# A planned attention and two-layer kernel: longer assumed delays for its loads, and the x2 stores of layer 1 begun by GpSimd

## The chip, the cores and the metric

The kernel runs on one core of a Trainium2 chip. The metric is the device time of one execution in microseconds. Engines are called as the profile calls them: PE is TensorE (matrix products), DVE is VectorE, ACT is ScalarE, POOL is GpSimd, SP is SyncE, which only begins transfers (DMAs).

## The reference

Causal attention in blocks of 64 rows over 4 batches, 8 heads, 576 positions and a head size of 64 gives 2304 tokens of 512 numbers. Two layers follow, each a product with a 512 x 2048 matrix, a function of each element, and a product with a 2048 x 512 matrix. All is in float32.

```python
scores = scale * np.matmul(q, k.transpose(0, 1, 3, 2))
mask = block_i >= block_j            # blocks of 64 positions
scores = np.where(mask, scores, -1000000000.0)
attn = np.exp(scores - np.max(scores, axis=-1, keepdims=True))
attn = attn / (np.sum(attn, axis=-1, keepdims=True) + 1e-09)
x = np.matmul(attn, v)               # then heads side by side: [2304, 512]
# layer 1
h = x @ moe_w_in
g = np.where(h >= 1, h, np.where(h <= -1, 0.0, (h + 1) ** 2 / 4))
x = g @ moe_w_out
# layer 2
h = x @ moe2_w_in
out = (h * np.cos(h)) @ moe2_w_out
```

## The kernel before

The work has three stages on PE: attention (to about 160 us), layer 1 (to 557 us), layer 2. Each float32 product of a layer is made of three products in a shorter form: an operand is split into a high and a low part (a copy that rounds, then a subtraction, the helpers cp and diff, lines 189 to 191 and 185).

Attention goes through 16 pairs of heads, in periods of two pairs. Q, K and V are loaded by SP, scores are computed in units (S3, S2, S0 and "tl" for the last 64 rows of two pairs), DVE takes the maximum (line 598) and prepares the divisor (lines 621 and 625), ACT the exponential, and POOL divides (line 635); PE turns the result (line 692) and multiplies it with V (line 727, then the halves, 738). Beside it the weights of layer 1 are brought in: a raw load of 512 KB, then two steps "top" and "low" (ACT, the second also on POOL, line 290), a joining step on DVE (line 300), and the split into the two parts in tile m or n. Ten of these conversions lie in attention, at pairs 6 to 15.

Layer 1 runs over five blocks of tokens (four of 512, and the third of 256), each in 16 steps over the hidden dimension. A step has a first product (mm1, line 868, into h), four operations on ACT and DVE that make g (881, 882, 883 and its split), and a second product (mm2, line 909) into four accumulators called parts 0 to 3. The first product is issued two steps ahead of the second. At a block's last step each part is copied to the tile o, which has two buffers taken in turn (part % 2), and stored to x2d in memory by two DMAs of 128 KB (for the block of 256: one of 256 KB, line 925). So part 2 can be copied only when both stores of part 0 have landed, part 3 only after those of part 1, and the next block's second product needs the part's accumulator empty. In the same stage the weights of layer 2 are converted (w_combine: raw loads, top, low, join, sums of pieces on line 340, and stores of tiles o and f to w2i and w2o), and x_load fetches the next block's x (line 839).

What decides the order of all this: PE's order is written out by hand (OPENING, PERIOD, CLOSING, and the loop over steps). All else is put into a Plan. An operation has a cost per engine on which it may run, what it reads and writes, and a latency until its result counts as there. The plan simulates the engines and gives each operation to the engine and place where it could begin first; the instructions are then issued in exactly that order, and each engine works through its own in order. So a number in the plan sets no wait of its own; it changes the order, and with costs for several engines ("AV", "AG") who does the work. Latencies of transfers were 2.0 us everywhere:

```python
    def dma(kb, reads, writes, fn):
        do("S", 0.1 + kb / 230.0, reads, writes, lambda e: fn(), latency=2.0)
```

Of the kernel before, what the change touches and what calls it, by code (L numbers as in the profile page):

```python
# [102 lines left out]
def attn_moe_moe_kernel(ctx: ExitStack, tc: tile.TileContext, q, k, v, w_in1, w_out1, w_in2, w_out2, out):  # L103
    nc = tc.nc
    B, H, S, D = q.shape
# [4 lines left out]
    NB = 256  # L110
# [8 lines left out]
    KB = 1024  # L119
    pin = tc.keep_in_program_order  # L120
# [47 lines left out]
    x2d = [dram.tile([DM, NB], F32, name=f"x2d{j}") for j in range(NBLK)]  # L168
# [33 lines left out]
    def do(eng, cost, reads, writes, fn, lock="G", latency=0.0):  # L202
        plan.add(eng, cost, reads, writes, fn, lock, latency)
# [9 lines left out]
    def dma(kb, reads, writes, fn):  # L213
        do("S", 0.1 + kb / 230.0, reads, writes, lambda e: fn(), latency=2.0)

    def issue(count, kb, reads, writes, fn, rate=270.0):
        do("S", max(0.45 * count, kb / rate), reads, writes, lambda e: fn(), latency=2.0)

    def span(name, off, size):
        return [(name, b) for b in range(off // 512, (off + size + 511) // 512)]  # L220
# [40 lines left out]
    def raw_load(layer, f, which, slot, after=()):  # L261

        def emit():
            a = M.F1.view((8 + 4 * slot) * KB, [2 * DM], I32)
            w = srcs[layer][which].bitcast(I32)
            start = load_in_order if after else nc.sync.dma_start
            if which == 0:
                start(
                    out=a.rearrange("p (k f) -> p k f", k=NK),
                    in_=w[:, f * 256:(f + 1) * 256].rearrange("(k p) f -> p k f", p=128),  # L270
                )
            else:
                start(out=a, in_=w[f * 128:(f + 1) * 128, :])

        (issue if after else lambda _, *args: dma(*args))(1, 512, list(after), [("top", slot), ("low", slot)] + span("f", (8 + 4 * slot) * KB, 4 * KB), emit)

    def joined(slot, v, vk):

# [122 lines left out]
    for n in range(NK, N):  # L401
        b, h, _ = pairs[n]
# [79 lines left out]
    def raw_keys(n, which, parts=range(2)):  # L482
        return [("raw", which, raw_home(n, which), a) for a in (parts if n < PE_PAIRS[which] else [n % 2])]

    def load_v(n):
        src, t, hs = v[pairs[n][0]], M.V[n % 2], heads(n)

        def emit():
            for h in range(2):
                load_in_order(  # L490
                    out=t[:, 0:LAST, h, :], in_=src[pairs[n][1 + h], 0:128 * LAST, :].rearrange("(t p) d -> p t d", p=128)
                )
            o = slice(64 * (n % 2), 64 * (n % 2) + 64)
            load_in_order(out=t[o, LAST], in_=src[hs, 128 * LAST:S, :].rearrange("h p d -> p h d"))
            for x in range(2):
                at_ = 256 * x + 128
                load_in_order(
                    out=t[64:128, LAST + 1 + x], in_=src[hs, at_:at_ + 64, :].rearrange("h p d -> p h d")
                )

        issue(5, 358, [], [("V", n % 2)], emit, 205.0)

    def load(n, which, part=None):
        if n >= N:
            return
        if which == 2:
            return load_v(n)
        b, h0, h1 = pairs[n]
        src = (k, q)[which][b]
        t = M.R[which][raw_home(n, which)]  # L510
        if n < PE_PAIRS[which]:
            parts = range(2) if part is None else [part]
            c = slice(NTK * parts[0], NTK * parts[-1] + NTK)

            def emit():
                for h in range(2):
                    load_in_order(
                        out=raw_view(n, which)[:, c, h, :], in_=src[pairs[n][1 + h]].rearrange("(t p) d -> p t d", p=TK)[:, c],
                    )

            issue(2, 147 * len(parts), [], raw_keys(n, which, parts), emit, 205.0)
            return

        def emit():
            for x in range(4):
                g = src[h0 + 2 * (x // 2):h0 + 2 * (x // 2) + 2].rearrange("h t d -> (h t) d")
                load_in_order(
                    out=t[32 * x:32 * x + 32].rearrange("p (a d) -> p a d", d=32),
                    in_=g[:, 32 * (x % 2):32 * (x % 2) + 32].rearrange("(a r) d -> r a d", r=32),
                )  # L530

        issue(4, 590, [], raw_keys(n, which) + raw_keys(n + 1, which), emit, 140.0)

    def load_next(n, which):
        p = PE_PAIRS[which]
# [353 lines left out]
    def mm2(s, part):  # L889
# [29 lines left out]
        cp("AV", 512, y, a_of, [A], Y)  # L919
        if two:  # L920
            for c, j in enumerate(js):
                dma(128, Y, [("x2d", j, part)], lambda c=c, j=j: nc.sync.dma_start(
                    out=x2d[j][128 * part:128 * (part + 1)], in_=y()[:, NB * c:NB * (c + 1)]))
        else:
            dma(256, Y, [("x2d", js[0], part)], lambda: nc.sync.dma_start(
                out=x2d[js[0]][256 * part:256 * (part + 1)].rearrange("(k p) n -> p k n", p=128),
                in_=y().rearrange("p (k n) -> p k n", k=2),
            ))

    HT = 384  # L930
    AT = ({1: 0, 2: 1, 4: 2, 6: 3, 3: 4, 7: 5, 5: 6}, {1: 0, 2: 1, 3: 2, 5: 3, 7: 4, 4: 5, 6: 6})
# [567 lines left out]
```

## Time and profile before

| | |
|---|---|
| time, median of 3 runs | 919.14 us (916.41 to 920.05) |
| profiled execution | 918.29 us, its span 916.5 us |
| PE busy | 905.4 us, 99% |
| DVE, ACT, POOL busy | 71%, 62%, 17% |
| DMA issues of the x2 stores | 34, all by SP |
| raw weight loads of 512 KB, issue to landing (median) | 4.4 and 4.7 us |
| loads of V of 128 KB; of K and of Q of 144 KB (median) | 2.7; 4.3 and 3.1 us |
| x2 stores of 128 KB (median) | 1.8 us |

The span runs from the first to the last instruction; the profiled execution's time is 1.8 us longer. Times in the rows are counted from the start of the span.

### The profile page before, as it was taken

How to read it: one execution, taken by the hardware profiler on the slowest of the kernel's cores; microseconds unless marked ns; L12 is line 12 of the kernel's file. 1: busy time of each engine (PE TensorE's matmuls, PEld its weight loads, DVE VectorE, ACT ScalarE, POOL GpSimd, SP SyncE). 2: the span in 40 equal slices, each digit the busy share in tenths (PEclk: the TensorE clock that was granted, in tenths of full speed). 3: DMA queues.
4: the chain of work that ended last, by engine and by line, in shares of the span. 5: the costliest groups of instructions: out<-in, count | busy, mean ns of one | idle time of the engine just before them, and what ended most of it. 6: DMA issues, size and time to landing. Idle time of an engine off the chain costs nothing.

```text
span 916.5 us, 17951 instructions
## 1 busy us (share of the span) xinstructions
PE 905.4 (99%) x6834; PEld 811.5 (89%) x6834; DVE 655.3 (71%) x1041; ACT 564.3 (62%) x1060; POOL 159.2 (17%) x279
## 2 busy tenths in 40 slices
PE   8999999999999999999999999999999999999998
PEld 6778778888878889988888889999999999999998
DVE  6799997777856666666336224999959899388883
ACT  6978887897757656566445334776417674166641
POOL 3567775332101101202000000000000000000000
PEclk9999999999999999999999999999999999999999
DMA  7769865875766575575230506777897777877771
GB/s 154 147 131 210 184 177 166 256 241 175 255 235 218 198 240 206 182 257 207 81 114 24 207 30 225 253 250 250 275 348 254 254 249 257 292 259 253 247 263 61
DMA packets 159957, 189.92 MB, mean 207 GB/s; under 512 B 84608, under 2 KB 117888, under 8 KB 159872
## 3 DMA queue, kind: packets, MB, share of 16 engines
q1 hardware_dynamic: 159872, 188.78, 64.4%
q8 instruction: 54, 0.88, 0.4%
q14 instruction: 31, 0.25, 0.1%
HBM read 145.23 MB, written 43.52 MB: 206 GB/s over the span
## 4 chain that ended last, share of the span: by engine, by line
PE 88%; DVE 4%; SPq 2%; DMA 2%; ACT 2%; issue 1%; POOL 1%; ACTq 0%; POOLq 0%; DVEq 0%
PE a L909 19%; PE h L868 19%; PE q L1052 19%; PE q L1153 18%; PE t L692 3%; PE t L589 3%; PE t L727 3%; PE end L1153 2%; SPq L839 1%; SPq L123 1%; PE t L784 1%; DVE sm L598 1%; PE t L738 1%; DVE n L194 1%; PE t L655 1%
## 5 line engine op out<-in xcount | busy, mean ns | idle before, releaser
L1052 PE MATMUL q<-m 128*128 128x384 f32 x1008 | 175.2, 334 | 0.0
L1052 PEld LDWEIGHTS q<-m 128*128 128x128 f32 x1008 | 174.7, 188 | 0.1
L1153 PE MATMUL q<-m,n 128*128 128x256 f32 x1116 | 136.5, 283 | 0.0
L1153 PEld LDWEIGHTS q<-m,n 128*128 128x128 f32 x1116 | 135.2, 192 | 0.0
L909 PE MATMUL a<-g,m 128*128 128x512 f32 (+1 forms) x540 | 120.8, 372 | 3.6 <-ACT o L189 2.3
L883 DVE SCALAR_TENSOR_TENSOR f<-f,h 128x512 f32<-128x512 f32 (+1 forms) x80 | 50.5, 631 | 91.8 <-ACT f L882 91.5
L909 PEld LDWEIGHTS a<-g,m 128*128 128x128 f32 x540 | 95.2, 190 | 22.0 <-ACT o L189 3.0
L881 ACT ACTIVATE f<-h,half 128x512 f32<-128x512 f32 (+1 forms) x80 | 51.3, 641 | 83.9 <-PE h L868 83.6
L185 DVE TENSOR_TENSOR g<-f,g 128x512 fp32r<-128x512 f32 (+1 forms) x80 | 54.2, 678 | 30.1 <-ACT g L189 25.3
L868 PE MATMUL h<-m 128*128 128x512 f32 (+1 forms) x324 | 66.8, 355 | 0.0
L189 ACT ACTIVATE g<-f 128x512 fp32r<-128x512 f32 (+1 forms) x71 | 42.6, 600 | 33.8 <-DVE f L883 33.8
L868 PEld LDWEIGHTS h<-m 128*128 128x128 f32 x324 | 54.1, 189 | 8.6
L598 DVE TENSOR_REDUCE sm<-t 128x1 f32<-128x384 f32 (+7 forms) x128 | 50.4, 447 | 13.4 <-PE t L589 12.8
L300 DVE SCALAR_TENSOR_TENSOR f<-f 128x512 uint32<-128x512 uint32 x64 | 45.3, 712 | 17.0 <-ACT f L285 15.0
L635 POOL TENSOR_SCALAR n<-n,sm 128x64 f32<-128x64 f32 (+6 forms) x104 | 49.3, 497 | 32.4 <-ACT n L668 14.0
L1021 ACT ACTIVATE f<-f,hpi 128x768 f32<-128x768 f32 x48 | 44.6, 929 | 16.3 <-DVE f L1017 16.3
L868 PE MATMUL h<-x,m 128*128 128x512 f32 x216 | 52.6, 391 | 0.0
L909 PE MATMUL a<-g,n 128*128 128x512 f32 (+1 forms) x240 | 52.5, 368 | 0.0
L909 PEld LDWEIGHTS a<-g,n 128*128 128x128 f32 x240 | 42.1, 189 | 7.5
L868 PEld LDWEIGHTS h<-x,m 128*128 128x128 f32 x216 | 40.7, 190 | 8.4
L882 ACT ACTIVATE f<-f 128x512 f32<-128x512 f32 (+1 forms) x80 | 46.9, 586 | 1.7
L285 ACT ACTIVATE f<-f 128x512 f32<-128x512 f32 x64 | 42.8, 675 | 0.5 <-DMA f<-in_moe_w_in_dram 0.4
(143 smaller groups left out, 1642.4 us busy)
## 6 DMA issues: line engine op xcount, KB each, us to landing
m<-w2i SPq DMA_DIRECT2D x84, 512.0 KB, 4.2
m<-w2o SPq DMA_DIRECT2D x84, 512.0 KB, 3.7
f<-in_moe_w_out_dram SPq DMA_DIRECT2D x32, 512.0 KB, 4.4
f<-in_moe_w_in_dram SPq DMA_DIRECT2D x32, 512.0 KB, 4.7
w2i<-f SPq DMA_DIRECT2D x8, 1024.0 KB, 4.3
w2o<-f SPq DMA_DIRECT2D x8, 1024.0 KB, 4.2
w2i<-o SPq DMA_DIRECT2D x8, 768.0 KB, 3.4
w2o<-o SPq DMA_DIRECT2D x8, 768.0 KB, 4.4
```

Of the source, the lines that this page charges most:

```text
L185: return (eng or nc.vector).tensor_tensor(out=lo, in0=raw, in1=hi.bitcast(F32), op=ALU.subtract)
L300: pin(nc.vector.scalar_tensor_tensor(out=v().bitcast(U32), in0=t.bitcast(U32), scalar=3, in1=w.bitcast(U32), op0=ALU.logical_shift_left, o ...
L598: nc.vector.tensor_reduce(out=stat(0, n, i, i + 1), in_=pb(at_, a)[:, off:off + nk], axis=AX.X, op=ALU.max, negate=True,)))
L635: do("G", 0.25 + 0.00082 * w, sk(2, n, e0, e0 + 1) + [P_(i, n)], [writes], lambda e: pin(nc.gpsimd.tensor_scalar(out=out(), in0=probs(i, m ...
L868: pin(nc.tensor.matmul(out=h_of(), lhsT=wt[:, a, kk * 128:(kk + 1) * 128], rhs=x[:, b, 0:w], start=(kk == 0 and i == 0), stop=(kk == NK - ...
L881: nc.scalar.activation(out=g(), in_=h_of(), func=ACTF.Relu, bias=half, scale=0.5)))
L882: do("A", 0.05 + 0.00084 * w, E, E, lambda e: pin(nc.scalar.activation(out=g(), in_=g(), func=ACTF.Square)))
L883: do("V", 0.07 + w / 960.0, [H] + E, E, lambda e: pin(nc.vector.scalar_tensor_tensor(out=g(), in0=g(), scalar=1.0, in1=h_of(), op0=ALU.min ...
L909: pin(nc.tensor.matmul(out=o, lhsT=wt[:, a, dm:dm + 128], rhs=b, start=(f == 0 and i == 0 and c == 0), stop=(f == NF - 1 and i == 2), skip ...
L1021: nc.scalar.activation(out=o, in_=a, func=func, **kw)
L1052: pin(nc.tensor.matmul(out=ps[:, e, 0:HT], lhsT=w[:, e, a, 128 * kk:128 * (kk + 1)], rhs=L2.xq[i][:, kk, c], start=(not src and kk == 0 an ...
L1153: pin(nc.tensor.matmul(out=part(m), lhsT=t[:, e, a, 128 * m:128 * (m + 1)], rhs=w[:, e, o], start=(i not in (2, 3) and q == 0 and e == 0 a ...
```

## The change

Four numbers of the plan change: the latency that it counts for attention's loads of V goes from 2.0 to 2.5, that for the later loads of K and Q (four DMAs for two pairs) from 2.0 to 3.0, and that for raw weight loads of layer 1 that wait for a mark in attention from 2.0 to 5.0. The stores of x2 are begun by POOL in place of SP; the plan counts 0.9 us of POOL for each and a latency of 2.0, and they are fixed in the plan's order, which the stores on SP were not. As after.py has four lines more, its line numbers are 4 higher from line 276 on.

```diff
--- before.py
+++ after.py
@@ -213,8 +213,8 @@
     def dma(kb, reads, writes, fn):
         do("S", 0.1 + kb / 230.0, reads, writes, lambda e: fn(), latency=2.0)
 
-    def issue(count, kb, reads, writes, fn, rate=270.0):
-        do("S", max(0.45 * count, kb / rate), reads, writes, lambda e: fn(), latency=2.0)
+    def issue(count, kb, reads, writes, fn, rate=270.0, latency=2.0):
+        do("S", max(0.45 * count, kb / rate), reads, writes, lambda e: fn(), latency=latency)
 
     def span(name, off, size):
         return [(name, b) for b in range(off // 512, (off + size + 511) // 512)]
@@ -272,7 +272,11 @@
             else:
                 start(out=a, in_=w[f * 128:(f + 1) * 128, :])
 
-        (issue if after else lambda _, *args: dma(*args))(1, 512, list(after), [("top", slot), ("low", slot)] + span("f", (8 + 4 * slot) * KB, 4 * KB), emit)
+        keys = [("top", slot), ("low", slot)] + span("f", (8 + 4 * slot) * KB, 4 * KB)
+        if after:
+            issue(1, 512, list(after), keys, emit, latency=5.0)
+        else:
+            dma(512, [], keys, emit)
 
     def joined(slot, v, vk):
 
@@ -498,7 +502,7 @@
                     out=t[64:128, LAST + 1 + x], in_=src[hs, at_:at_ + 64, :].rearrange("h p d -> p h d")
                 )
 
-        issue(5, 358, [], [("V", n % 2)], emit, 205.0)
+        issue(5, 358, [], [("V", n % 2)], emit, 205.0, 2.5)
 
     def load(n, which, part=None):
         if n >= N:
@@ -529,7 +533,7 @@
                     in_=g[:, 32 * (x % 2):32 * (x % 2) + 32].rearrange("(a r) d -> r a d", r=32),
                 )
 
-        issue(4, 590, [], raw_keys(n, which) + raw_keys(n + 1, which), emit, 140.0)
+        issue(4, 590, [], raw_keys(n, which) + raw_keys(n + 1, which), emit, 140.0, 3.0)
 
     def load_next(n, which):
         p = PE_PAIRS[which]
@@ -919,13 +923,13 @@
         cp("AV", 512, y, a_of, [A], Y)
         if two:
             for c, j in enumerate(js):
-                dma(128, Y, [("x2d", j, part)], lambda c=c, j=j: nc.sync.dma_start(
-                    out=x2d[j][128 * part:128 * (part + 1)], in_=y()[:, NB * c:NB * (c + 1)]))
+                do("G", 0.9, Y, [("x2d", j, part)], lambda e, c=c, j=j: pin(nc.gpsimd.dma_start(
+                    out=x2d[j][128 * part:128 * (part + 1)], in_=y()[:, NB * c:NB * (c + 1)])), latency=2.0)
         else:
-            dma(256, Y, [("x2d", js[0], part)], lambda: nc.sync.dma_start(
+            do("G", 0.9, Y, [("x2d", js[0], part)], lambda e: pin(nc.gpsimd.dma_start(
                 out=x2d[js[0]][256 * part:256 * (part + 1)].rearrange("(k p) n -> p k n", p=128),
                 in_=y().rearrange("p (k n) -> p k n", k=2),
-            ))
+            )), latency=2.0)
 
     HT = 384
     AT = ({1: 0, 2: 1, 4: 2, 6: 3, 3: 4, 7: 5, 5: 6}, {1: 0, 2: 1, 3: 2, 5: 3, 7: 4, 4: 5, 6: 6})
```

PE's instructions stand in the same order before and after. On the other engines the order is the same up to about pair 8 of attention and differs from there. Three places matter below.

The first is POOL in attention, behind the division of a tail row (n<-n,sm 128x576), some 107 us into the span: line 635 (639 after) divides, line 290 is the "low" step of a raw weight, lines 191 and 185 split a weight into m. Before:

```order
L290 TENSOR_SCALAR f<-f 128x512
L635 TENSOR_SCALAR P_119<-P_119,sm 128x384
L635 TENSOR_SCALAR P_119<-P_119,sm 128x512
L635 TENSOR_SCALAR P_119<-P_119,sm 128x320
L635 TENSOR_SCALAR P_119<-P_119,sm 128x64
L635 TENSOR_SCALAR P_119<-P_119,sm 128x384
L635 TENSOR_SCALAR P_119<-P_119,sm 128x128
L635 TENSOR_SCALAR P_119<-P_119,sm 128x256
L635 TENSOR_SCALAR P_119<-P_119,sm 128x128
L635 TENSOR_SCALAR P_119<-P_119,sm 128x64 x2
L191 TENSOR_SCALAR m<-f 128x512 x2
L185 TENSOR_TENSOR m<-f,m 128x512 x2
```

After, from the division n<-n,sm 128x576 on:

```order
L639 TENSOR_SCALAR n<-n,sm 128x576
L639 TENSOR_SCALAR P_119<-P_119,sm 128x384
L639 TENSOR_SCALAR P_119<-P_119,sm 128x512
L639 TENSOR_SCALAR P_119<-P_119,sm 128x320
L639 TENSOR_SCALAR P_119<-P_119,sm 128x64
L639 TENSOR_SCALAR P_119<-P_119,sm 128x384
L639 TENSOR_SCALAR P_119<-P_119,sm 128x128
L639 TENSOR_SCALAR P_119<-P_119,sm 128x256
L639 TENSOR_SCALAR P_119<-P_119,sm 128x128
L639 TENSOR_SCALAR P_119<-P_119,sm 128x64 x2
L191 TENSOR_SCALAR m<-f 128x512
L185 TENSOR_TENSOR m<-f,m 128x512
```

No step of line 290 stands ahead of the divisions of P any more, and the two copies and two subtractions that followed them without a pause are now one of each. (The same four of line 191 and 185 in a row stood two periods earlier too, 79.42 to 83.48; there they are now parted by five divisions.)

The second is DVE at the end of layer 1's first block. The names a_2948, a_2954 and a_2967 are accumulator parts 0, 1 and 3 (ACT copies part 2, a_2961). Before:

```order
L883 SCALAR_TENSOR_TENSOR f<-f,h_3570 128x512
L340 TENSOR_TENSOR f<-f 128x256 x2
L185 TENSOR_TENSOR g<-f,g 128x512
L185 TENSOR_TENSOR f<-f 128x2x256 x2
L194 COPY o<-a_2948 128x512
L194 COPY o<-a_2954 128x512
L883 SCALAR_TENSOR_TENSOR f<-f,h_3615 128x512
L300 SCALAR_TENSOR_TENSOR f<-f 128x512
L185 TENSOR_TENSOR g<-f,g 128x512
L300 SCALAR_TENSOR_TENSOR f<-f 128x512
L185 TENSOR_TENSOR o<-f,o 128x256
L185 TENSOR_TENSOR o<-f,o 128x2x256
```

After, a_2947, a_2953 and a_2961 are parts 0, 1 and 2, and ACT copies part 3, after the activations of h_3642:

```order
L304 SCALAR_TENSOR_TENSOR f<-f 128x512
L887 SCALAR_TENSOR_TENSOR f<-f,h_3557 128x512
L185 TENSOR_TENSOR g<-f,g 128x512
L304 SCALAR_TENSOR_TENSOR f<-f 128x512
L194 COPY o<-a_2947 128x512
L194 COPY o<-a_2953 128x512
L887 SCALAR_TENSOR_TENSOR f<-f,h_3601 128x512
L185 TENSOR_TENSOR g<-f,g 128x512
L194 COPY o<-a_2961 128x512
L185 TENSOR_TENSOR o<-f,o 128x2x256
L887 SCALAR_TENSOR_TENSOR f<-f,h_3642 128x512
```

The copies stand before the two subtractions f<-f of the weights' work, where they stood behind them, and DVE has the third part too.

The third is POOL at the same place after the change (before, it held no stores):

```order
L191 TENSOR_SCALAR g<-f 128x512
L191 TENSOR_SCALAR o<-f 128x256
L926 DMA x2d_64<-o 128x256
L926 DMA x2d_65<-o 128x256
L926 DMA x2d_64<-o 128x256
L926 DMA x2d_65<-o 128x256
L185 TENSOR_TENSOR o<-f,o 128x256
L926 DMA x2d_64<-o 128x256
L191 TENSOR_SCALAR g<-f 128x512
L926 DMA x2d_65<-o 128x256
```

The first four stores are those of parts 0 and 1; a copy of g, the high part of an operand of PE's second product, stands among those of parts 2 and 3. At the end of layer 1 POOL holds nothing but the last sixteen stores. On SP, x_load's sixteen loads at the second boundary now stand ahead of one store to w2i and two raw loads.

## Rows read from the trace of the kernel before

**Rows 1.** The page: busy time, share and instructions of TensorE.

```profile
PE 905.4 (99%) x6834; PEld 811.5 (89%) x6834; DVE 655.3 (71%) x1041; ACT 564.3 (62%) x1060; POOL 159.2 (17%) x279
```

**Rows 2.** Who waited for whom, TensorE's first row: us, times, longest.

```profile
PE a L909 <- ACT o L189: 2.3, 1, 2.3
```

**Rows 3.** Timeline of PE, attention: first product of P and V in three periods.

```profile
83.86 2.00 PE L727 MATMUL t<-n,rv 128*64 128x128 f32 x40
...
101.59 2.00 PE L727 MATMUL t<-n,rv 128*64 128x128 f32 x40
...
121.46 2.00 PE L727 MATMUL t<-n,rv 128*64 128x128 f32 x40
```

**Rows 4.** Timeline of all engines, 103 to 123 us, attention: start us, us, what.

```profile
109.35 0.67 POOL L290 TENSOR_SCALAR f<-f 128x512 uint32<-128x512 uint16 x1 [2.60 <-DMA f<-in_moe_w_in_dram]
...
115.47 1.20 POOL L191 TENSOR_SCALAR m<-f 128x512 fp32r<-128x512 f32 x2
...
115.57 3.59 DVE L621 TENSOR_SCALAR sm<-sm 128x4 f32<-128x4 f32 x1
...
116.64 2.48 POOL L185 TENSOR_TENSOR m<-f,m 128x512 fp32r<-128x512 f32 x2
...
120.34 1.19 PE L655 MATMUL t<-K,Q 64*64 64x288 f32 x12 [1.24 <-DVE n L194]
```

**Rows 5.** Line 621 in the whole run: duration ns min/median/max, first and last start.

```profile
L621 DVE TENSOR_SCALAR sm<-sm x48: 108/160/3587, 14.0 to 149.6; 128x4 f32<-128x4 f32 x32, 128x1 f32<-128x1 f32 x16
```

**Rows 6.** Timeline of PE at the first block boundary of layer 1.

```profile
251.39 1.52 PE L909 MATMUL a<-g,m 128*128 128x512 f32 x6
252.75 1.52 PE L868 MATMUL h<-x,m 128*128 128x512 f32 x6
256.56 2.93 PE L909 MATMUL a<-g,m 128*128 128x512 f32 x6 [2.29 <-ACT o L189]
...
260.94 1.30 PE L909 MATMUL a<-g,m 128*128 128x512 f32 x5
```

**Rows 7.** Busy time by engine in one stretch, then clock, DMA share, GB/s.

```profile
240.00:260.00 20.00, 17.71 (x71) 14.09 (x71) 16.87 (x31) 13.20 (x24) 2.70 (x5) 0.91 0.87 299
```

**Rows 8.** Timeline of the other engines at the first block boundary.

```profile
248.21 1.29 DVE L185 TENSOR_TENSOR f<-f 128x512 fp32r<-128x512 f32 x2
...
249.42 1.28 DVE L194 COPY o<-a 128x512 f32<-128x512 f32 x2
...
250.13 3.05 SPq L922 DMA_DIRECT2D x2d<-o  x4
...
255.92 0.58 ACT L189 ACTIVATE o<-a 128x512 f32<-128x512 f32 x1
```

**Rows 9.** Line 922, the x2 stores: all issues to landing.

```profile
DMA to landing us min/median/max: 1.7/1.8/5.5
```

**Rows 10.** Timeline at the second block boundary of layer 1.

```profile
336.46 0.63 ACT L189 ACTIVATE x<-x 128x512 fp32r<-128x512 f32 x1 [1.87 <-DMA x<-x1d]
...
343.07 1.60 PE L868 MATMUL h<-m 128*128 128x256 f32 x12
...
344.45 0.60 ACT L189 ACTIVATE o<-a 128x512 f32<-128x512 f32 x1 [4.02 <-DMA x2d<-o]
...
345.95 1.60 PE L868 MATMUL h<-m 128*128 128x256 f32 x12
...
353.75 1.60 PE L868 MATMUL h<-m 128*128 128x256 f32 x12
```

**Rows 11.** Timeline at the end of layer 1 and the start of layer 2.

```profile
555.68 3.70 SPq L922 DMA_DIRECT2D x2d<-o  x6
...
558.95 0.60 ACT L189 ACTIVATE o<-a 128x512 f32<-128x512 f32 x1 [0.38 <-DMA x2d<-o]
559.44 0.81 ACT L1067 ACTIVATE f<-q 128x768 f32<-128x768 f32 x1
...
561.35 0.96 DVE L1070 TENSOR_TENSOR w<-q,f 128x768 f32<-128x768 f32 x1 [8.95 <-PE q L1052]
```


## Prediction

> **What bounds the kernel now.** The page's busy times come first: TensorE (PE) is busy 905.4 of 916.5 us [rows 1], so 11.1 us at most are idle, and no edit here takes a matmul away. The order of PE's instructions is in fact the same after the change, row for row. What can move is only what PE waits for. The list of PE's waits names where: the longest is 2.3 us, once, for a ScalarE (ACT) copy out of an accumulator [rows 2]. An idle figure understates such a stop, since the modelled ends of matmuls cover part of it and the clock may fall behind it. So I took losses from starts, by comparing a stretch with its undisturbed neighbour in the timeline of PE. There are three:
>
> Attention. The first product of P and V starts at 83.86, 101.59 and 121.46 in three periods of the same work [rows 3]: 17.73 us, then 19.87, so 2.1 us are lost in the second. The place is the tail scores at 120.34, released by a VectorE (DVE) copy [rows 4]. That copy is late because one tiny DVE instruction, line 621 on 128x4, lasts 3.59 us against a median of 0.16 [rows 4, 5], exactly while GpSimd (POOL) runs two conversion copies and two subtractions without a pause, 115.47 to 119.12. POOL itself is late there: it stood 2.60 us waiting for a raw weight load before 109.35, with ten divisions of P behind it [rows 4].
>
> First block boundary of layer 1, 254 us. Undisturbed, half a product (six matmuls) takes 252.75 - 251.39 = 1.36 us, so the half starting at 260.94, three halves behind the one at 252.75, was due at 256.83: 4.1 us lost [rows 6]. 2.29 of it is the wait; the six matmuls after it take 2.93 us instead of 1.52, which is the lower clock level, 1.2 in place of 2.4 GHz, after the stop, and the stretch shows a mean granted clock of 0.91 [rows 6, 7]. What PE waited for is the third accumulator part, copied out by ACT at 255.92; the first two parts were copied by DVE at 249.42, behind two other subtractions at 248.21 [rows 8].
>
> Second boundary, 344 us. Two products there take 345.95 - 343.07 = 2.88 us; twice that after 345.95 is 351.71, and the row stands at 353.75: 2.0 us lost [rows 10]. ACT sat 4.02 us at the third part's copy until a store of the first part had landed, and all later activations stood behind it [rows 10].
>
> **The change, part by part.** *Longer delays.* They add no instruction; they make the plan order users of a load later. In attention POOL no longer has a raw-weight step ahead of its divisions, so the 2.60 us wait has nothing to hold, and the run of two copies and two subtractions is half as long. At most the whole 2.1 us comes back, at least nothing, if ACT or DVE, which take over work, wait for the load instead. I take -1.7: both things the rows blame are gone in the new order, but small losses stay everywhere.
>
> *First boundary.* In the new order DVE takes parts one to three, ahead of the two subtractions (1.29 us [rows 8]), and ACT only the fourth. The third part must be free when PE comes to it at 254.11 (252.75 + 1.36), the fourth 0.68 later. A store issued by POOL has no row in this trace. I take the plan's own figures, 0.9 us to issue and 2.0 to land, which are near the stores' median of 1.8 from SyncE (SP) [rows 9]; their slowest, 5.5, is the other end. If DVE copies at 248.1, the first store can begin at 248.8. The second, on which the third part's buffer hangs, lands at 248.8 + 1.8 + 2.0 = 252.6, and the copy ends 0.64 later, in time. The fourth store lands at 248.8 + 3.6 + 2.0 = 254.4, and its copy ends at 255.0: 0.2 late. If DVE is as late as now (249.42, stores from 250.1), the fourth lands at 255.7 and PE stops about 1.5 us, without the clock loss if that needs a stop like the present one. So 2.6 to 3.9 us come back; I take -3.4. Behind POOL's waiting stores stands one copy of g, wanted by PE two products later (at 262), so that costs nothing unless the stores take twice as long.
>
> *Second boundary.* The new order puts all sixteen loads of x before the 1 MB weight store and two raw loads on SP; POOL copies the last piece of x, at 336.46 as ACT does now [rows 10], and issues the stores from 337.1. The second lands at 337.1 + 1.8 + 2.0 = 340.9, and ACT's copy can end at 341.5 where it now starts at 344.45. PE needs what follows it at 347.39 (345.95 + 1.44). All 2.0 us come back, or, with a landing of 5.5 (344.4), nothing; I take -1.7.
>
> The Trainium skill's page "DMA: Bandwidth & Descriptors", section "Issuing engines are not separate DMA queues", speaks against this term: DMAs begun on different engines share the same 16 DMA engines, and another issuer saves only issue time. By that rule the landing stays slow wherever the bytes are, and the sum would be 1.7 us higher. The row agrees with it as far as it goes: the 5.5 us is a landing, not an issue [rows 9].
>
> *End of layer 1.* This is the price. The four copies out of the accumulators, all on ACT, are unchanged in order, and ACT's first copy for layer 2 stands behind them. SP begins the stores at 555.68; ACT's fourth copy runs at 558.95, as soon as its buffer's stores have landed; the layer 2 copy runs 559.44 to 560.25; PE wants it at about 561.3, when the second product ends and releases DVE [rows 11]. So there is 1 us in hand. With POOL the fourth store lands at 555.68 + 3.6 + 2.0 = 561.3, the copy (0.60) ends at 561.9, the next (0.81) at 562.7: PE stops 1.5 us where it does not stop now. If POOL is as quick as SP it costs nothing; with landings of 5.5 us it ends at 566.2, 5 us plus the clock. I take +1.5.
>
> The Trainium skill's page "SBUF — State Buffer", section "SBUF: two separate sides", warns that descriptors of a DMA issued from GpSimd cannot be written while DVE holds the shared port in a two-port copy between SBUF tiles. At this place it would add nothing, since DVE has been idle for 8.95 us [rows 11]; at the first boundary DVE's copies read PSUM. That one can wait for the other's port is what the 3.59 us of line 621 look like [rows 4].
>
> *At nothing.* SP loses 34 issues; POOL gains 34 x 0.9 = 31 us but is busy only 159.2 [rows 1]. Six more copies of g on POOL hide behind the two products by which the first matrix product runs ahead; without that cover each costs its wait.
>
> **Sum.** -1.7 - 3.4 - 1.7 + 1.5 = -5.3 us. The profiled execution took 918.29 us (its span is 916.5), so 913.0. It lies 0.85 below the median of the runs shown, 919.14.
>
> **Rivals.** *One of the three losses stays.* ACT's fourth copy at the first boundary stands behind an activation that is now done at 254.3; if ACT is as late again, or a reordered weight step makes a new stop of that size, the 3.4 us are not won: 916.4. For it speaks that every wait here came from steps that the plan had placed too early, and it still counts 2.0 us for layer 2's raw loads; against it, that the copies come before that work now. Chance 0.31.
>
> *The edits move nothing that PE feels:* the stops return at other places in the same size, 918 to 919. Chance 0.06.
>
> *The stores are slow from POOL, and the kernel gets slower.* One mechanism: issue plus landing of a store. At the first boundary (late case) the fourth part would be freed later by every microsecond that a landing takes beyond 2.0, and at the end of layer 1 too, and once the stop there passes the 2.29 us seen, the clock loss of some 1.7 us comes with it. That happens at a landing of 2.8 (1.5 + 0.8), from which on the gains are used up. With 5.5, the fourth part is freed at 259.8 (5 us late, 6.7 with the clock, 2.6 more than now), the end costs 6.7, the second boundary gains nothing: 918.3 - 1.7 + 2.6 + 6.7 = 925.9. Against it: a median of 1.8 in 32 stores [rows 9]. Chance 0.08.
>
> **How the numbers follow.** The forecast has 0.55. Its own best case is everything won and no price at the end: 918.3 - 2.1 - 4.1 - 2.0 = 910.1. The range reaches from 909.9 to 918.2, where both boundaries would be as before but for attention's gain and the price at the end (918.3 - 1.7 + 1.5 = 918.1). About 0.5% (4.6 us) is what a measurement of this kernel can tell from no change; faster than that means below 914.5. The forecast gives nearly all of 0.55 to it, and the first rival a little: faster 0.55, same 0.37, slower 0.08.
>
> **What would show it.** Right: no POOL wait for a raw load before the divisions near 107 us and periods of about 17.7 us throughout; at the first boundary PE stopping for less than 1.5 us with a granted clock of 1.00; no 4 us wait of ACT at the second boundary; and a new PE wait of 1 to 2 us about 4 us into layer 2, released by ACT's or DVE's first copies there. Wrong: a store from POOL that takes over 2.8 us to land, or a stop of over 2 us at any other block boundary.

## The result and the profile after

The changed kernel takes 911.71 us (median of 4, 910.97 to 912.26), the kernel before 919.6 on the same chip (median of 4, 916.41 to 920.23): 0.9901 of its time, 95% interval 0.9872 to 0.9929. So it is about 1% faster, and 913.0 was forecast. The profiled execution took 911.95 us (span 910.1), 6.34 less than the one of before.

TensorE's row of the page after, the first of its waits (us in total, times, longest), and busy time and granted clock (1.00, the higher of the two levels) at the first boundary; they answer to [rows 1, 2, 7]:

```profile
PE 903.0 (99%) x6834; PEld 811.8 (89%) x6834; DVE 651.0 (72%) x1040; ACT 564.2 (62%) x1052; POOL 188.2 (21%) x322
```

```profile
PE t L816 <- DVE f L1338: 1.0, 1, 1.0
```

```profile
240.00:260.00 20.00, 20.00 (x89) 16.54 (x89) 13.45 (x24) 13.52 (x23) 7.40 (x13) 1.00 0.64 229
```

The wait of 2.3 us for an accumulator's copy is gone, and no product of layer 1 stands in the list; its longest wait is 1.0 us. The timeline of PE at the first boundary, and under it that of the engines that copy and store the parts:

```profile
251.16 1.52 PE L913 MATMUL a<-g,m 128*128 128x512 f32 x6
252.52 1.52 PE L872 MATMUL h<-x,m 128*128 128x512 f32 x6
253.88 1.52 PE L913 MATMUL a<-g,m 128*128 128x512 f32 x6
...
256.60 2.88 PE L913 MATMUL a<-g,m 128*128 128x512 f32 x12
```

```profile
246.60 1.37 DVE L194 COPY o<-a 128x512 f32<-128x512 f32 x2 [0.66 <-PE a L913]
...
247.60 2.35 POOL L926 DMA_DIRECT2D x2d<-o  x4
...
252.05 0.69 DVE L194 COPY o<-a 128x512 f32<-128x512 f32 x1 [0.77 <-DMA x2d<-o]
```

Five halves start 1.36 us apart (the fourth, at 255.24, is left out above): all 4.1 us of [rows 6] are won. VectorE copies the first two parts at 246.60, as soon as PE releases them; the third part is free at 252.74, wanted at 253.88. At the second boundary the rows of PE run on at 1.44 us where [rows 10] lose 2.0:

```profile
338.72 1.60 PE L872 MATMUL h<-m 128*128 128x256 f32 x12
...
347.36 1.60 PE L872 MATMUL h<-m 128*128 128x256 f32 x12
```

The loads of x, the copies of parts and the stores at that boundary, before:

```profile
324.16 10.04 SPq L839 DMA_DIRECT2D x<-x1d  x16
...
337.73 0.68 DVE L194 COPY o<-a 128x512 f32<-128x512 f32 x1
...
338.44 2.88 SPq L922 DMA_DIRECT2D x2d<-o  x4
```

and after:

```profile
319.81 10.05 SPq L843 DMA_DIRECT2D x<-x1d  x16
...
331.11 0.69 DVE L194 COPY o<-a 128x512 f32<-128x512 f32 x1 [0.48 <-PE a L913]
...
332.58 2.20 POOL L926 DMA_DIRECT2D x2d<-o  x4
...
337.73 0.60 ACT L189 ACTIVATE o<-a 128x512 f32<-128x512 f32 x1 [1.30 <-DMA x2d<-o]
```

PE itself is 4.35 us ahead there (the product at 338.72 is the one at 343.07 in [rows 10]). With that taken off, the loads of x begin where they began (324.16 - 4.35 = 319.81). What comes earlier are the copies of the first two parts, by 2.3 us, the stores, by 1.5, and the copy of the third part, by 2.4 (344.45 in [rows 10]).

At the end of layer 1, where a new stop of 1.5 us was forecast, there is none:

```profile
549.35 2.13 POOL L926 DMA_DIRECT2D x2d<-o  x4 [74.53 <-ACT o L189]
550.30 5.91 PE L1056 MATMUL q<-m 128*128 128x384 f32 x33
...
553.50 0.81 ACT L1071 ACTIVATE f<-q 128x768 f32<-128x768 f32 x1
554.76 0.96 DVE L1074 TENSOR_TENSOR w<-q,f 128x768 f32<-128x768 f32 x1 [8.95 <-PE q L1056]
```

ACT's first copy for layer 2 begins 3.20 us behind PE's first product of layer 2 (550.30), where it began 2.54 behind it (559.44 - 556.90): 0.66 us of the 1 us in hand are used. Nothing is late: VectorE's first subtraction there begins when PE releases it, after 8.95 us without work.

In attention GpSimd's wait of 2.60 us for a raw weight [rows 4] is gone, and the timeline near 120 us reads:

```profile
108.78 4.33 POOL L639 TENSOR_SCALAR P<-P,sm 128x384 f32<-128x384 f32 x10 [1.62 <-DVE sm L629]
...
112.70 2.42 PE L731 MATMUL t<-n,rv 128*64 128x128 f32 x40
...
115.89 1.15 DVE L625 TENSOR_SCALAR sm<-sm 128x4 f32<-128x4 f32 x1
...
119.80 1.20 PE L659 MATMUL t<-K,Q 64*64 64x288 f32 x16 [0.63 <-DVE n L194]
```

The tiny DVE instruction (now line 625) lasts 1.15 us where it lasted 3.59, and the tail scores wait 0.63 us instead of 1.24. But layer 1's first boundary is reached at 251.16 instead of 251.39, only 0.2 us earlier. Where the gain lies is counted next.

To compare runs I use two numbers of PE's timeline throughout. **Attention** is the start of the half product at the first boundary (251.39 before, 251.16 after). **Layer 1** is the time from there to the first product of layer 2 (556.90 - 251.39 = 305.51 before, 550.30 - 251.16 = 299.14 after). By the two profiles 6.6 us are won up to layer 2, 0.2 in attention and 6.4 in layer 1; layer 2 itself takes the same to 0.2 us (916.5 - 556.90, 910.1 - 550.30).

Both numbers come from one profiled execution of each kernel. Attention holds a part that is not the edit's: the first product of P and V starts at 28.18 before, 28.36 after and in delays_only, 28.96 in pool_in_sp_place, 29.22 in sp_in_pool_place, 29.26 in raw_2_05 and 29.95 in delays_v5. The kernel after and sp_in_pool_place have the same rows there and differ by 0.9 us. So differences in attention below 1 us say little.

### The profile page after: what moved, and what is told of

Same layout as the page of the kernel before. It is cut to its first block, busy times and chain, and to the rows that moved or that the text cites. A ratio compares the mean times of both kernels' runs of the same rounds, so it can differ in the third digit from the quotient of the medians.

```text
span 910.1 us, 17990 instructions
## 1 busy us (share of the span) xinstructions
PE 903.0 (99%) x6834; PEld 811.8 (89%) x6834; DVE 651.0 (72%) x1040; ACT 564.2 (62%) x1052; POOL 188.2 (21%) x322
## 4 chain that ended last, share of the span: by engine, by line
PE 94%; DVE 2%; DMA 1%; SPq 1%; POOL 1%; issue 0%; ACT 0%; POOLq 0%; DVEq 0%
PE h L872 22%; PE a L913 22%; PE q L1056 19%; PE q L1157 18%; PE t L696 3%; PE t L731 3%; PE t L593 3%; PE end L1157 2%; DMA rv<-in_v_dram 1%; SPq L123 1%; DVE n L194 1%; PE t L788 1%; PE t L659 1%; DVE sm L602 1%; PE t L742 1%; POOL n L639 1%
## 5 line engine op out<-in xcount | busy, mean ns | idle before, releaser
L913 PE MATMUL a<-g,m 128*128 128x512 f32 (+1 forms) x540 | 118.7, 368 | 0.0
L189 ACT ACTIVATE g<-f 128x512 fp32r<-128x512 f32 (+1 forms) x68 | 40.1, 590 | 30.1 <-DVE f L887 30.0
```

The costliest lines, as they stand in the source:

```text
L913: pin(nc.tensor.matmul(out=o, lhsT=wt[:, a, dm:dm + 128], rhs=b, start=(f == 0 and i == 0 and c == 0), stop=(f == NF - 1 and i == 2), skip ...
```

## The experiments

The first theory (A) was the prediction's: layer 1's boundaries are won, and by the stores: they leave SyncE's queue, or the plan gives them a better place. Its rival (B) was that the longer delays do it and the stores only ride along.

| run | ratio to before (95%) | median us (lowest to highest, runs) | attention | layer 1 |
|---|---|---|---|---|
| before (own profile) | 1 | 921.05 (917.36 to 924.36, 23), beside the first four | 251.39 | 305.51 |
| after | 0.9901 (0.9872 to 0.9929) | 911.71 (910.97 to 912.26, 4) | 251.16 | 299.14 |
| stores_only | 0.9961 (0.9943 to 0.998) | 916.96 (913.58 to 920.16, 12) | 254.12 | 303.00 |
| delays_only | 0.9907 (0.9882 to 0.9932) | 911.85 (911.08 to 913.11, 6) | 251.49 | 299.14 |
| sp_in_pool_place | 0.9908 (0.9883 to 0.9932) | 912.26 (911.32 to 912.54, 6) | 251.81 | 299.14 |
| pool_in_sp_place | 1.0026 (1.0005 to 1.0046) | 923.83 (920.13 to 926.82, 12) | 256.03 | 308.31 |
| raw_only | 0.9911 (0.9896 to 0.9927) | 913.21 (912.34 to 913.81, 6) | 251.36 | 300.44 |
| vkq_only | 0.9933 (0.9914 to 0.9953) | 914.73 (913.13 to 918.23, 6) | 251.63 | 301.56 |
| raw_8 | 0.9935 (0.9919 to 0.995) | 915.09 (914.12 to 916.0, 6) | 251.13 | 301.60 |
| l2raw_only | 0.9947 (0.9926 to 0.9968) | 916.04 (914.25 to 918.9, 6) | 252.19 | 300.64 |
| two_copies_early | 0.9977 (0.9957 to 0.9997) | 916.49 (912.94 to 919.61, 12) | 251.33 | 301.96 |
| raw_2_05 | 0.9953 (0.9936 to 0.997) | 914.39 (912.83 to 915.87, 12) | 253.97 | 299.39 |
| raw_2_4 | 0.9966 (0.995 to 0.9981) | 914.85 (913.4 to 918.65, 12) | 251.01 | 302.04 |
| delays_v5 | 1.0005 (0.9988 to 1.0022) | 918.89 (916.84 to 920.26, 12) | 257.83 | 299.64 |

Each four rows below after were timed beside runs of before of their own, with medians of 921.05, 920.92 and 918.6, the last four on another chip: times are compared by ratio.

**Stores alone.** The change without its delays:

```diff
-            issue(1, 512, list(after), keys, emit, latency=5.0)
+            issue(1, 512, list(after), keys, emit)
...
-        issue(5, 358, [], [("V", n % 2)], emit, 205.0, 2.5)
+        issue(5, 358, [], [("V", n % 2)], emit, 205.0)
...
-        issue(4, 590, [], raw_keys(n, which) + raw_keys(n + 1, which), emit, 140.0, 3.0)
+        issue(4, 590, [], raw_keys(n, which) + raw_keys(n + 1, which), emit, 140.0)
```

> The stores move to GpSimd, all delays stay as before (2.0). Theory A (the 6 us come from layer 1's boundaries, and there from the stores alone): both boundaries run without a stop, attention keeps its stop near 120 us, 912 us. Rival B (the longer delays shift the order, and the stores only ride along): the boundaries keep most of their 4.1 and 2.0 us, 916 to 919 us.

It won less than half. The first boundary is nearly clean, but at the second a stop larger than that of before stands (PE's timeline of this run; from 344.80 to 350.09 are 5.29 us where two steps of 1.44 are due):

```profile
344.80 1.60 PE L872 MATMUL h<-m 128*128 128x256 f32 x12
...
348.30 1.99 PE L913 MATMUL a<-g,m 128*128 128x256 f32 x11 [0.56 <-DVE g L185]
350.09 2.72 PE L872 MATMUL h<-m 128*128 128x256 f32 x12
```

**Delays alone.** The change with its stores taken back:

```diff
-                do("G", 0.9, Y, [("x2d", j, part)], lambda e, c=c, j=j: pin(nc.gpsimd.dma_start(
-                    out=x2d[j][128 * part:128 * (part + 1)], in_=y()[:, NB * c:NB * (c + 1)])), latency=2.0)
+                dma(128, Y, [("x2d", j, part)], lambda c=c, j=j: nc.sync.dma_start(
+                    out=x2d[j][128 * part:128 * (part + 1)], in_=y()[:, NB * c:NB * (c + 1)]))
```

> The three longer delays, with the stores begun by SyncE as before. Theory A: at the first boundary VectorE's third copy stands behind two further pairs of subtractions and the stores stand among 1 MB weight stores, so both stops of layer 1 come back in about their old size, 917 to 919 us. Rival B: 912 to 913 us.

Theory A falls: 911.85 us, and layer 1 takes 299.14 us, to the hundredth what it takes after. I had read from the order that VectorE's third copy would be late behind subtractions; the timeline shows it waiting 0.39 us for the first part's stores, with all four operations of line 344 done, and ending ahead of 254.21, when PE wants the part:

```profile
247.65 1.90 SPq L926 DMA_DIRECT2D x2d<-o  x4
...
251.38 1.30 DVE L344 TENSOR_TENSOR f<-f 128x256 f32<-128x256 f32 x2
...
253.06 0.69 DVE L194 COPY o<-a 128x512 f32<-128x512 f32 x1 [0.39 <-DMA x2d<-o]
```

**Only who begins the stores.** Two runs hold the order of TensorE, VectorE and ScalarE row for row and change the issuer alone: the change with SyncE at GpSimd's places, and the kernel before with GpSimd at SyncE's.

```diff
-                do("G", 0.9, Y, [("x2d", j, part)], lambda e, c=c, j=j: pin(nc.gpsimd.dma_start(
+                do("G", 0.9, Y, [("x2d", j, part)], lambda e, c=c, j=j: pin(nc.sync.dma_start(
...
-                dma(128, Y, [("x2d", j, part)], lambda c=c, j=j: nc.sync.dma_start(
+                dma(128, Y, [("x2d", j, part)], lambda c=c, j=j: nc.gpsimd.dma_start(
```

> The changed kernel's order on TensorE, VectorE and ScalarE, row for row, but SyncE begins the stores, at the place that the plan gave them on GpSimd. Theory A1 (the order, in which VectorE copies three parts and all of x is loaded first, is what wins): 912 to 913 us, no stop above 1 us. Theory A2 (SyncE's queue is what cost the time, since a store waits there among 1 MB weight stores): half or more of the 6 us are lost again, 915 to 918 us, and ScalarE or VectorE wait over 3 us for a store at a boundary.

> The kernel before, its order on TensorE, VectorE and ScalarE row for row, but GpSimd begins the stores where SyncE did. Theory A1 (order): the third part is still copied too late at the first boundary and the last x comes late at the second, 917 to 919 us or more, since GpSimd's own work now holds up stores too. Theory A2 (queue): the store that ScalarE waited 4.02 us for lands some 2 us earlier, and so the third part at the first boundary, 913 to 915 us.

The issuer is worth nothing in the new order (912.26 against 911.71, both 0.991 of before; layer 1 the same 299.14) and costs a little in the old one. Theory A2 falls, and A1 is what remains of A: an order of VectorE's and ScalarE's rows, in which stores are in time from either engine. The time from issue to landing of the first four stores at the first boundary, and then of the first four at the second, for SyncE in the new order:

```profile
DMA to landing us min/median/max: 3.6/3.8/4.0
```

```profile
DMA to landing us min/median/max: 4.2/4.7/5.0
```

and for GpSimd in the kernel after, with the issue times of all 32:

```profile
DMA to landing us min/median/max: 3.2/3.5/4.0
```

```profile
DMA to landing us min/median/max: 4.0/4.4/4.9
```

```profile
L926 POOL DMA_DIRECT2D x2d<-o x32: 540/540/728, 247.6 to 554.4; - x32
```

The same stores at the same places take nearly the same time from either engine; over all 32 the medians are 2.7 and 2.8 us. The kernel before was no faster: 2.9 to 3.7 us at the first boundary and 4.5 to 5.5 at the second. Its median of 1.8 [rows 9] comes from the later boundaries, where the first four stores land in 1.7 to 1.8 us each. The rule of the Trainium skill's page "DMA: Bandwidth & Descriptors" (section "Issuing engines are not separate DMA queues"), that another issuer saves issue time alone, agrees with that; a single issue is not shorter either, with GpSimd's 0.54 us a store against 0.42 in SyncE's median.

The second of these runs showed something else. Attention took 256.03 us, 4.6 more than in the profile of before, with the same rows in the same order there. Its timeline, PE's, GpSimd's, VectorE's and SyncE's rows:

```profile
68.90 2.42 SPq L123 DMA_DIRECT2D x1d<-xs  x2
71.37 0.43 SPq L123 DMA_DIRECT2D f<-in_moe_w_out_dram  x1
...
75.96 0.67 POOL L290 TENSOR_SCALAR f<-f 128x512 uint32<-128x512 uint16 x1 [3.63 <-DMA f<-in_moe_w_out_dram]
...
76.72 5.39 POOL L635 TENSOR_SCALAR P<-P,sm 128x384 f32<-128x384 f32 x10
...
77.61 1.62 PE L589 MATMUL t<-K,Q 64*64 64x256 f32 x24 [1.18 <-ACT n L189]
...
82.18 3.58 DVE L621 TENSOR_SCALAR sm<-sm 128x4 f32<-128x4 f32 x1
```

and the same places of the kernel before:

```profile
67.24 1.17 SPq L123 DMA_DIRECT2D x1d<-xs  x2
68.46 0.64 SPq L123 DMA_DIRECT2D f<-in_moe_w_out_dram  x1
...
73.00 0.67 POOL L290 TENSOR_SCALAR f<-f 128x512 uint32<-128x512 uint16 x1 [1.45 <-DMA f<-in_moe_w_out_dram]
73.75 4.35 POOL L635 TENSOR_SCALAR P<-P,sm 128x384 f32<-128x384 f32 x10
```

SyncE came to two stores of x1 1.66 us later and took 2.42 us to issue them instead of 1.17, so the raw weight behind them was issued at 71.37 instead of 68.46. The load itself took about 4.5 us in both (75.96 - 71.37, 73.00 - 68.46). In the one execution that gave GpSimd 1.45 us of waiting and PE none; in the other 3.63, the ten divisions 3 us late, a stop of PE for ScalarE, which stood before a raw weight too, and the 3.58 us of the tiny instruction. The same happened to stores_only (2.33 us for the two stores, attention 254.12). In raw_2_05 the two stores took 1.32 us, but SyncE was late by 1.5 already, with the same end. The profile of before was a good draw of a lottery; two_copies_early, with the same order in attention, drew 251.33.

**Which delay.** With the stores on SyncE again: raw weights alone (5.0), V, K and Q alone, raw weights alone at 8.0, and the kernel before with 5.0 for layer 2's raw weights alone.

```diff
-            dma(512, [], keys, emit)
+            do("S", 0.1 + 512 / 230.0, [], keys, lambda e: emit(), latency=5.0)
```

(the last of the four; the others set the three numbers of the change).

> Of the change only the raw weights' delay of 5.0 us; V, K and Q and the stores as before. Theory C (this delay alone does it: in attention GpSimd no longer waits for a raw weight with ten divisions behind, and at the boundaries the steps on weights stand behind the copies of parts): 911 to 913 us, no GpSimd wait for a raw weight above 1 us in attention, no stop at layer 1's first two boundaries. Rival D (the 6 us need all three delays together, since each only shifts the order a little): 914 to 918 us.

> Of the change only the delays of V (2.5) and of the later K and Q (3.0); raw weights 2.0 and the stores as before. Theory C: the waits of GpSimd for raw weights near 75 and 107 us stay with their stops, and layer 1 loses 3 to 6 us at its boundaries, 917 to 921 us. Rival D: part of the gain, 914 to 917 us.

> As the run with the raw weights' delay alone, but 8.0 us instead of 5.0. Theory C (a delay at or above the time that a raw weight really takes puts its users where they don't hold an engine up): again 911 to 913 us. Rival E (5.0 only happens to shift layer 1's steps to a good place, and another delay shifts them to a bad one): a stop of 1.5 to 4 us at one of layer 1's boundaries, 914 to 917 us, with attention as good as with 5.0.

> The kernel before with 5.0 us counted for layer 2's raw weights, whose conversion runs beside layer 1's products, instead of 2.0; layer 1's raw weights, V, K, Q and the stores as before. If layer 1's stops come from steps on these weights that stand ahead of the copies of parts because their loads are counted too short, both stops go, 913 to 915 us, with attention as before. If they come from attention's delays, which set where layer 1's steps fall, or from luck of the order: 917 us or more.

No theory of one right delay survives. All four are faster than before, those that leave the raw weights of layer 1 at 2.0 too, and each takes another time for layer 1: 300.44, 301.56, 301.60, 300.64. The run with layer 2's raw weights met neither of its two forecasts: its first boundary is clean, and at the second a stop of 1.5 us stays (two products take 4.38 us, from 342.63 to 347.01, where 2.88 are due). At the third boundary, where PE waits for no copy in the kernel after, a stop stands in raw_only (the first fence) and a longer one in raw_8:

```profile
385.74 1.64 PE L913 MATMUL a<-g,m 128*128 128x512 f32 x6 [1.00 <-DVE o L194]
```

```profile
386.67 1.66 PE L913 MATMUL a<-g,m 128*128 128x512 f32 x6 [1.46 <-ACT o L189]
```

That is rival E for layer 1. For attention there is one sign of theory C: the scatter. With 6 runs each, vkq_only and l2raw_only (raw weights at 2.0) spread over 5.1 and 4.7 us, and delays_only, raw_only and raw_8 over 2.0, 1.5 and 1.9.

**Two copies, moved by hand.** In the kernel before, the plan's order is kept but for two instructions, which are written out as soon as what they need has been:

```diff
+        for i in sorted(self.early):
+            pair = self.seq.pop(next(k for k, (j, _) in enumerate(self.seq) if j == i))
+            self.seq.insert(1 + max(k for k, (j, _) in enumerate(self.seq) if j in self.ops[i][1]), pair)
...
+        plan.early |= {len(plan.ops)} if (kb, part) in ((0, 2), (0, 3)) else set()
         cp("AV", 512, y, a_of, [A], Y)
```

> The kernel before with two instructions moved: at layer 1's first boundary ScalarE's copy of the third part stands ahead of four instructions and VectorE's copy of the fourth ahead of four, and their stores directly behind the first four on SyncE; every other row as before. If the stop of 4.1 us comes from those two queues (steps on weights ahead of the copies), the half products run through there at 1.36 us each, and the kernel is 3 to 4 us faster than before, with attention and the second boundary (2.0 us) as before. If the copies only wait for the stores instead, the stop keeps 1.5 us or more.

The first boundary in its timeline:

```profile
252.69 1.52 PE L868 MATMUL h<-x,m 128*128 128x512 f32 x6
253.66 0.60 ACT L189 ACTIVATE o<-a 128x512 f32<-128x512 f32 x1 [1.76 <-DMA x2d<-o]
...
254.31 1.91 PE L908 MATMUL a<-g,m 128*128 128x512 f32 x6
```

The half product starts at 254.31, 0.26 behind its due time (252.69 + 1.36), where it started at 256.56 before. Layer 1 takes 301.96, 3.55 us less, about the 4.1 of this stop; the 2.0 of the second boundary are not in it. So the first stop was the two engines' queues, with no load counted otherwise and no store on GpSimd. (On SyncE one store of weights also moved, behind the four stores of parts 2 and 3.) The time fell by 0.23% (0.03 to 0.43); 3.55 us would be 0.39%, inside that interval.

**A delay that can't matter.** Raw weights alone at 2.05 and at 2.4.

> The raw weights' delay counted 2.05 us instead of 2.0, nothing else of the change: too little to matter for any wait, but enough to reorder some rows. If layer 1's gain is right timing in the plan (Theory C): as before, 917 to 921 us, with both stops. If layer 1's order before was an unlucky one of many (Rival E): the sum of its stops changes by more than 1.5 us, most likely down (914 to 917 us), while attention keeps its GpSimd waits for raw weights and its scatter from run to run.

> As the run with 2.05 us, but 2.4: a second draw of the order. Theory C: 917 to 921 us. Rival E: again another sum of stops in layer 1, 913 to 918 us, and attention as before.

Changing one number by 0.05 us wins 6.12 of the 6.37 us of layer 1 (299.39). PE's first boundary in that run, and GpSimd in its attention:

```profile
253.97 1.52 PE L913 MATMUL a<-g,m 128*128 128x512 f32 x6
255.32 1.52 PE L872 MATMUL h<-x,m 128*128 128x512 f32 x6
256.69 1.55 PE L913 MATMUL a<-g,m 128*128 128x512 f32 x6
```

```profile
75.22 0.69 POOL L294 TENSOR_SCALAR f<-f 128x512 uint32<-128x512 uint16 x1 [2.60 <-DMA f<-in_moe_w_out_dram]
```

The halves start 1.35 and 1.37 us apart, and attention is 2.6 us later than in the profile of before (1.1 of it at 28 us already), with GpSimd's wait for a raw weight and the long tiny instruction (3.59 us at 81.45) in it. Its scatter was forecast to stay, but its twelve runs spread over 3.0 us, where the twelve of two_copies_early beside them spread over 6.7. For layer 1 this answers the question: the order before was an unlucky one, and every other order that a change of a delay gave here was better, by 3.47 us (with 2.4) to 6.37.

**V counted longer still.** The three delays with 5.0 for V, to win the rest of attention.

> The three longer delays with the stores on SyncE, and V counted 5.0 us instead of 2.5, since the first products with P and V of two periods still wait for V. If V alone holds attention up there, those periods come back to 17.5 us and the kernel takes 911 to 911.5 us where it took 911.9. If the new order brings a stop in layer 1, 913 us or more.

Neither: attention lost 6.3 us against delays_only (257.83), layer 1 kept 299.64. In three periods PE now waits 0.85 us for a division that stands later, as here, and 1.84 at the end, besides 0.86 for ScalarE at 140.26:

```profile
84.11 0.74 PE L696 MATMUL t<-ident,P 128*128 128x128 f32 x5 [0.85 <-POOL n L639]
...
164.20 1.15 PE L788 MATMUL t<-n,rv 128*64 128x64 f32 x32 [1.84 <-DVE n L194]
```

Of the 6.3 us 1.6 are there at 28 us already (29.95 against 28.36); the waits named come to 5.2 us, against waits in delays_only that are gone here, and the balance was not drawn up. The two first products of P and V that were thought to wait for V take 2.00 us here (at 79.31 and 116.73). So longer is not better by itself.

## Why the prediction was right, and where it was not

**The sum** was right (913.0 for 911.7), and the three places of loss were the right ones: 6.1 of the 6.6 us that the profiles show lie at the first two boundaries. That the sum came so near is in part luck: by the profiles attention gave 1.5 us less than forecast, and the end of layer 1 cost 1.5 less. The terms were not of the right size, and the reason given for the largest two was wrong in part.

**First boundary, -3.4 forecast, -4.1 measured.** The step that held is that the parts must be copied ahead of the steps on weights: two copies moved by hand give 3.55 of it. What failed is what the step took for granted, that the stores on GpSimd are a part of the mechanism: the same time is had with SyncE (delays_only, sp_in_pool_place). The landing was mis-sized too. The forecast took it from a median of 1.8 [rows 9] that mixes busy and quiet boundaries and counted 2.9 us for a store, issue and landing together; the first four took 3.2 to 4.0. What made up for it: VectorE's copies ran at 246.60, 1.3 us ahead of the early case of 248.1 (PE itself is 0.2 ahead), and an issue took 0.54 us instead of 0.9.

**Second boundary, -1.7 forecast, -2.0 measured.** Here too the copies of the first two parts come earlier in the new order; the loads of x, on which the term laid weight, begin and end where they did beside PE's work. The first four stores took 4.0 to 4.9 us with their issue, where the sum had 2.9 and the case without any gain 6.4 (0.9 + 5.5), and the gain came all the same: the third part is copied 2.4 us earlier than before. The stores' issuer again plays no part; the term rested on it. That the copies' place is the cause is read from two timelines; no run moves these copies alone.

**Attention, -1.7 forecast, -0.2 by the profiles** (-0.4 counted from the first product of P and V). GpSimd's wait and most of the 3.59 us are gone as forecast, and the period that ends at 121.46 [rows 3] takes 18.94 us instead of 19.87 (120.94 - 102.00). But two others got longer, from 17.48 to 17.93 and from 17.96 to 18.25; the first product of P and V takes 2.32 us at 77.06 and 2.42 at 112.70 where 2.00 is undisturbed, while SyncE is still issuing V's loads (106.20 to 114.16). With V counted longer (delays_v5) these products take 2.00 again, but other waits came in their place, so what V alone costs is not settled. The mis-sized step is that I took one execution for the kernel. Its loss there was 2.1 us at one place; other executions of the same order lost 2.7 and 4.6 us more (stores_only, pool_in_sp_place), 0.2 and 0.8 of that ahead of 28 us. Over the medians of the chip, 919.6 - 911.71 = 7.9 us are won, and 6.37 of these are layer 1, which leaves about 1.5 for attention. That is an estimate, close to the term, but the interval of the ratio (6.5 to 11.8 us) leaves anything from 0.2 to 5.4. What the runs show of the scatter: after, delays_only, sp_in_pool_place, raw_only and raw_8, in whose profiles GpSimd waits for no raw weight from 60 to 150 us, spread over 1.2 to 2.0 us in 4 to 6 runs each, the other eight changed kernels over 3.0 to 6.7 in 6 or 12. Among the eight is delays_v5, which counts 5.0 for raw weights and waits 1.93 us for one all the same: it is the waits that go with the scatter, not the number by itself. The two groups nearly touch (standard deviations of 0.78 us in delays_only and 0.80 in raw_2_05), and no run takes the waits alone away.

**End of layer 1, +1.5 forecast, 0 measured.** The mis-sized term is the issue: 0.9 us a store was taken from the plan, 0.54 measured, so the four are issued in 2.13 us instead of 3.6. The landing was quicker than counted too, 2.0 us with the issue instead of 2.9. Together that is more than the price.

**The signs.** The clock stayed at 1.00 at the first boundary and ScalarE waits 1.30 us instead of 4 at the second, as named for a right forecast; periods of 17.7 us throughout and the new wait in layer 2 did not come. The first sign of a wrong one, a store that takes over 2.8 us to land, did come, and cost nothing.

**The rivals.** That one of the losses stays (0.31) is what stores_only, raw_only, raw_8 and raw_2_4 show: a change of the plan's numbers can leave or make a stop anywhere, and this change happened not to. The stop that costs the whole gain (0.08) did not come, although at the first boundary the stores landed about as late as it asked for (2.6 to 3.3 us behind their issue, against 2.8): its bound stood on copies as late as before and on 0.9 us of issue four times.

**Better than both.** No run beat the changed kernel measurably. The stores on GpSimd can be left out of it at no cost.

**Open.** Why SyncE's two stores take 1.17 us to issue in one execution and 2.42 in another was not tried, nor what sets the landing at 2 us or at 4 to 5; nor how the remaining stops of layer 1 are avoided by rule and not by luck, for instance by a due time for the copies of parts.

## What to carry to other kernels

When a planner sets the order, a change of any of its numbers is a new draw of the whole order: run a change of the same number that can't matter before crediting the edit with what it wins, and hold the order fixed when one part is to be priced. Look at several executions, not at one profile, where an engine with work queued behind it waits for a load: what such a wait cost here was drawn anew in each execution, and the kernels without such waits scattered least. Take a transfer's time from the place where it counts: a median over the whole run said 1.8 us where the stores that mattered took 3 to 5.

## What was not expected of the hardware

A DVE instruction on 128x4, 0.16 us in the median, lasted 3.58 to 3.61 us once in each of before, stores_only, pool_in_sp_place (there 3.18 once more), l2raw_only and raw_2_05. Each time it began with GpSimd's back-to-back run of two copies and two subtractions [rows 4] and ended with the last of the four (115.57 + 3.59 = 119.16, against 116.64 + 2.48 = 119.12, in the kernel before). Where it began elsewhere it was shorter: its longest was 1.15, 0.75, 0.67 and 0.58 us in after, delays_only, raw_only and raw_8, and 0.58, 1.21 and 1.19 in vkq_only, two_copies_early and raw_2_4, which count raw weights at 2.0 or 2.4. So the long case goes with this meeting, and that comes or not with the execution: two_copies_early has the order of before there.

The first four stores of x2 at a boundary took 2.9 to 5.5 us from issue to landing at the first two boundaries and 1.7 to 2.0 at the last two, from either issuer (before, after, sp_in_pool_place).

A store of 128 KB occupies GpSimd for 0.54 us with hardly any scatter (540/540/728 ns), where SyncE's issue of the same store ran from 0.32 to 1.23 us before.
